# One copy of the last block's tail behind the join of the branches, and a new order in the one-lane block, in a fused WKV and two-layer mixture-of-experts kernel

## The chip, the cores and the metric

The kernel runs on one core of a Trainium2 chip. The metric is the device time of one execution in microseconds (us). The engines are called TensorE (PE in the profile, with its weight loads as PEld), VectorE (DVE), ScalarE (ACT), GpSimd (POOL) and SyncE (SP); the last two issue the transfers here, GpSimd those with indices (gathers and scatters) and SyncE the plain ones.

## What is computed

A recurrent attention gives one row per token; two mixture-of-experts (MoE) layers follow, each token going to the expert with the largest logit. The second layer has a capacity of 384 tokens per expert.

```python
# attention: B=2, H=8, S=768, D=48
for t in range(S):
    y[:, :, t] = einsum('bhd,bhde->bhe', rt, state + einsum('bhd,bhe->bhde', u * kt, vt))
    state = wt[..., None] * state + einsum('bhd,bhe->bhde', kt, vt)
x = y.transpose(0, 2, 1, 3).reshape(1536, 384)
# layer 0 (N=1536, D=384, E=8, F=1024)
logits = x @ w_gate + modality_bias[modality_id]
e = argmax(logits); gate = softmax(logits)[e]
x = gate * (relu(x @ w1[e]) @ w2[e])
# layer 1, without the bias, and with 384 places per expert
logits = x @ w_gate
e = argmax(logits); gate = softmax(logits)[e]
out = gate * (relu(x @ w1[e]) @ w2[e])   # 0 where the expert is full
```

## The kernel before

**Blocks.** In each layer a routing step sorts the tokens by expert into at most 13 blocks (NU) of two lanes of 128 rows. A block gathers its rows (`xg`), transposes them (`xp`, then the parts `xh` and `xl`), multiplies them with one expert's w1, takes the relu, multiplies with w2 into `y` (one PSUM tile per lane, `ykeep`), scales by the gate into a buffer `yo`, and scatters the rows to DRAM with an indirect DMA. Weights and activations are each split in two parts (h and l, `hi` at L960 and `lo` at L963) and three products are summed. The weights of block j+1 (`w1r`, `w2r` raw; `w1h`, `w1l`, `w2h`, `w2l` split) are split during block j: the high parts on ScalarE, the low parts on VectorE.

**Two forms.** A block whose two lanes share an expert has the form `two`; a block in which only its second lane has work has the form `one`. Here layer 0 has eight blocks: 0 to 5 are of form `two`, 6 and 7 of form `one`. Layer 1 has ten. The order of the work is written out by hand and is the same on each engine's queue; for `one` the table ONE lists by letters what stands behind which step: a to j are the pieces of the next block's weights (ScalarE and VectorE), `0` and `1` the relus of the two halves of F, `x` and `X` the transposes and casts of the next block's rows, `P` and `Q` the gate's softmax, and for the previous block's second lane `y` the transposes of its scaled row, `z` the two splits on VectorE, `l` its logits for layer 1 and then its store. The table RELU says on which engine the relu of each half runs.

**The outputs of layer 0.** A stored row of layer 0 holds the 384 values and 8 logits for layer 1's gate, which `yturn3`, `ysplit3` and `ylog3` work out from the scaled row. The second lane of block j is scaled, turned and stored only in block j+1 (from j = 5 on the scaling is the first ScalarE work of block j+1, L1127). The two buffers `yo` alternate with j.

**The end of layer 0.** How many blocks there are is known only at run time. `rest(j)` is a chain of tests: if there are more than j blocks, `body(j)` and `rest(j+1)`, else `last(j-1)`. Each of the possible ends has its own copy of `last`: a load of all rows' logits (`lgd`, L1337) on SyncE behind the stores, the load of layer 1's w2 of one expert (`w2r`, L913), the scaling of the last lane (L1343), its transposes (L1347), the copies (L1348), the logits (L696), a one-hot product that places them among the others (L1350, L1351), the store, and the add that gives layer 1's logits (L1354):

```python
nc.vector.tensor_add(lgs[1], lgs[0], pl)
```

Layer 1's routing starts from that sum, and its first gather needs the routing's result.

Of the kernel before, what the change touches and what calls it, by code (L numbers as in the profile page):

```python
# [27 lines left out]
E, F = 8, 1024  # L28
# [899 lines left out]
class MoePools:  # L928
    def __init__(self, tc, ctx, raw, run):
# [21 lines left out]
        self.gm = cp.tile([P, 2, 2], F32, name="gm")  # L951


def moe(tc, c, m, route, run, layer, src, w1d, w2d, dst, wg2, wp2, zb, following, lgs=None, psum=None, bad=None, general=None, ykeep=None):
# [21 lines left out]
    with ctx:  # L976
# [46 lines left out]
        def gates(j, part):  # L1023

            gd = m.gd[j % 2]
            if part == 0:
                lx = m.xg[j % 2][:, :, DM:XW]
                nc.vector.tensor_reduce(m.gm[:, 0], lx, AX.X, ALU.max)
                nc.vector.tensor_tensor(gd[:, :, 0:E], lx, m.gm[:, 0].unsqueeze(2).to_broadcast((P, 2, E)), ALU.subtract)  # L1029
            elif part == 1:  # L1030
                nc.scalar.activation(gd[:, :, 0:E], gd[:, :, 0:E], AF.Exp)
            else:

                nc.vector.tensor_reduce(m.gm[:, 1], gd, AX.X, ALU.add)
                nc.vector.reciprocal(R.gate[:, 2 * j : 2 * j + 2], m.gm[:, 1])
# [21 lines left out]
        def relu(j, half):  # L1057
# [3 lines left out]
            for a in range(0, 512, wd):  # L1061
                if RELU[half] == "s" or wd == 512:
# [61 lines left out]
        def scale(j, t, eng):  # L1124
            py = ykeep[t]
            if eng == "s":
                nc.scalar.activation(m.yo[j % 2][:, t, 0:DM], py, AF.Identity, scale=R.gate[:, 2 * j + t : 2 * j + t + 1])  # L1127
                return
            nc.vector.tensor_scalar(m.yo[j % 2][:, t, 0:DM], py, R.gate[:, 2 * j + t : 2 * j + t + 1], None, ALU.mult)

        def store(j, t):
            nc.gpsimd.indirect_dma_start(  # L1132
                out=dst, out_offset=bass.IndirectOffsetOnAxis(ap=R.ids[:, 2 * j + t : 2 * j + t + 1], axis=0),
                in_=m.yo[j % 2][:, t, 0:SO], in_offset=None, bounds_check=N - 1, oob_is_err=False,
            )

        def yturn3(j, t):
            pt = psum.tile([P, KD, P], F32, tag="tp", name=f"yt{j}{t}" + n, bufs=TP[layer])
            for kc in range(KD):
                nc.tensor.transpose(pt[:, kc], m.yo[j % 2][:, t, kc * P : (kc + 1) * P], c.ident)  # L1140
# [8 lines left out]
        def ylog3(j, t):  # L1149
            logits3(tc, psum, [m.yp], wp2, m.yo[j % 2][:, t : t + 1, DM:XW], f"_y{j}{t}" + n, "lg", 1)  # L1150
# [14 lines left out]
        def one(j, pc):  # L1165
# [3 lines left out]
            def work():  # L1169
                for p in next(plan):  # L1170
# [3 lines left out]
                    elif p == "y":  # L1174
                        if before:
                            if j < NU_MIN:
# [10 lines left out]
                    elif p == "s":  # L1187
                        if layer == 0 and j < NU_MIN - 1:
# [32 lines left out]
        def two(j, pc):  # L1221
            before = layer == 0 and j > 0
            first2(j, 0)
            if before:
                if j < NU_MIN:
# [44 lines left out]
            end = layer == 0 and j >= NU_MIN - 1  # L1270
# [3 lines left out]
            if layer == 0 and not end:  # L1274
# [48 lines left out]

        def last(j):
            if layer:
                finish(j)
            else:

                sp = ap.tile([P, 512], F32, tag="h0", name=f"sp{j}" + n, bufs=1)
                ohp, ohc = sp[:, 0:P], sp[:, P : P + NC]  # L1330
                put = sp[:, P + NC : P + NC * (E + 1)].rearrange("p (c e) -> p c e", e=E)
                col = slice(2 * j + 1, 2 * j + 2)
                nc.vector.tensor_scalar(ohp, c.i1[:, :, 0], R.tp[:, col], None, ALU.is_equal)
                nc.vector.tensor_scalar(ohc, c.jx[:, 0:NC], R.tc[:, col], None, ALU.is_equal)

                pl = psum.tile([P, NC, E], F32, tag="tp", name=f"lq{j}" + n, bufs=TP[0])
                nc.sync.dma_start(lgs[0], dst.rearrange("(p j) e -> p j e", j=NC)[:, :, DM:XW])  # L1337
                er = EXPERT0[j % 2]
                m.raw.load(j % 2, *following, slice(er, er + 1), parts=(1,))

                for kc in range(KD):
                    ks = slice(kc * P, kc * P + P)
                    nc.scalar.activation(m.yo[j % 2][:, 1, ks], ykeep[1][:, ks], AF.Identity, scale=R.gate[:, col])  # L1343
                xT = ap.tile([P, KD, P], F32, tag="lxT", name=f"lx{j}" + n, bufs=1)
                for kc in range(KD):
                    pt = psum.tile([P, P], F32, tag="h" if kc == 1 else "tp", name=f"yt{j}{kc}" + n, bufs=2 if kc == 1 else TP[0])
                    nc.tensor.transpose(pt, m.yo[j % 2][:, 1, kc * P : (kc + 1) * P], c.ident)  # L1347
                    nc.scalar.copy(xT[:, kc], pt)  # L1348
                py = logits(tc, psum, [xT[:, kc] for kc in range(KD)], wg2, None, None, f"_y{j}1" + n, "lg", 1)
                nc.vector.tensor_tensor(put, py.unsqueeze(1).to_broadcast((P, NC, E)), ohc.unsqueeze(2).to_broadcast((P, NC, E)), ALU.mult)  # L1350
                nc.tensor.matmul(pl, lhsT=ohp, rhs=put, start=True, stop=True)  # L1351
                nc.vector.tensor_copy(m.yo[j % 2][:, 1, DM:XW], py)
                store(j, 1)
                nc.vector.tensor_add(lgs[1], lgs[0], pl)  # L1354

                if j % 2 == 0:
                    for p in p0:
                        hi(p, nc.scalar)
                        lo(p, nc.vector)

        def rest(j):
# [140 lines left out]
```

## Time and profile before

| | |
|---|---|
| median of 3 runs | 452.43 us (452.07 to 452.55) |
| the profiled execution's own time | 451.07 us |
| its span, first to last instruction | 449.3 us |
| TensorE busy | 417.9 us, 93% |
| VectorE busy | 329.5 us, 73% |
| ScalarE busy | 249.3 us, 55% |
| layer 0's last block: first scaling, add behind it | 252.49 us, 273.28 us |

The times of single instructions come from the profiled execution, whose own time stands beside its span; the runs were timed without a profile. Blocks 6 and 7 of layer 0 lie between about 241 and 266 us.

### The profile page before, as it was taken

What the parts mean: (1) busy time and instruction counts of PE and PEld (TensorE: products, weight loads), DVE (VectorE), ACT (ScalarE), POOL (GpSimd) and SP (SyncE); (2) the same over time, 40 slices, a digit from 0 to 9 for tenths busy, and PEclk for the clock granted to TensorE, in tenths of its full rate; (3) what the DMA queues carried; (4) which work ended last, traced back from release to release, by engine and by line L of the source; (5) the groups of instructions that cost most, each with busy time, mean ns of one, the idle gap of its engine ahead of it and who ended that gap; (6) DMA issues with size and microseconds to landing.
All of it is one profiled execution on the core that took longest, in us unless ns stands there. A gap on an engine that the chain in (4) does not pass through costs nothing. (4 is left out here: it accounts for less than half of the span.)

```text
span 449.3 us, 9663 instructions
## 1 busy us (share of the span) xinstructions
PE 417.9 (93%) x3270; PEld 380.1 (85%) x3275; DVE 329.5 (73%) x677; ACT 249.3 (55%) x508; POOL 143.3 (32%) x160
## 2 busy tenths in 40 slices
PE   8999999999899999999999956999999999999990
PEld 4789988987389999999997854899899999998990
DVE  7798867984879859677597975386974945859760
ACT  3256545543537647557475840277864755777650
POOL 5637963141230422213223300503343132124420
PEclk9999999999899999999999996999999999999996
DMA  6987237348630121366744945314887657761100
GB/s 113 200 148 152 48 56 194 74 169 324 197 91 2 56 79 54 109 205 222 256 147 134 292 129 154 91 20 131 319 281 258 228 187 232 237 230 52 50 22 20
DMA packets 85590, 66.98 MB, mean 149 GB/s; under 512 B 60586, under 2 KB 77655, under 8 KB 85504
## 3 DMA queue, kind: packets, MB, share of 16 engines
q1 hardware_dynamic: 80512, 52.30, 39.8%
q0 software_dynamic: 4992, 13.61, 9.9%
q8 instruction: 44, 0.72, 0.7%
q14 instruction: 42, 0.34, 0.2%
HBM read 95.63 MB, written 11.56 MB: 239 GB/s over the span
## 5 line engine op out<-in xcount | busy, mean ns | idle before, releaser
L963 DVE TENSOR_TENSOR w1l<-w1r,w1h 128x512 fp32r<-128x512 f32 x114 | 71.7, 686 | 9.6 <-ACT w1h L960 9.4
L963 DVE TENSOR_TENSOR w2l<-w2r,w2h 128x768 fp32r<-128x768 f32 x76 | 69.2, 951 | 0.3 <-ACT w2h L960 0.3
L960 ACT CAST w1h<-w1r 128x512 fp32r<-128x512 f32 x114 | 62.7, 617 | 0.3 <-DMA xs<-zv 0.3
L1107 DVE SCALAR_TENSOR_TENSOR qhl_m<-qh_m,qhh_m 128x512 fp32r<-128x512 f32 x48 | 33.0, 686 | 36.0 <-ACT qhh_m L1106 36.0
L960 ACT CAST w2h<-w2r 128x768 fp32r<-128x768 f32 x76 | 59.4, 835 | 0.0
L1106 ACT ACTIVATE qhh_m<-qh_m 128x512 fp32r<-128x512 f32 x48 | 28.8, 599 | 41.7 <-PE qh_m L1101 41.7
L1101 PE MATMUL qh_m<-xh,w1h 128*128 128x256 f32 x288 | 51.0, 286 | 0.3 <-ACT xh L1318 0.2
L1101 PE MATMUL qh_m<-xl,w1h 128*128 128x256 f32 x288 | 50.2, 283 | 0.6 <-DVE w2l L963 0.6
L1119 PE MATMUL y_m<-w2h,qhh_m 128*128 128x384 f32 x192 | 50.0, 341 | 0.0
L1101 PE MATMUL qh_m<-xh,w1l 128*128 128x256 f32 x288 | 49.8, 282 | 0.0
L1119 PE MATMUL y_m<-w2l,qhh_m 128*128 128x384 f32 x192 | 49.6, 339 | 0.0
L1119 PE MATMUL y_m<-w2h,qhl_m 128*128 128x384 f32 x192 | 49.3, 338 | 0.0
L1004 POOL DMA_INDIRECT xg<-x,idg_l x24 | 26.0, 1083 | 69.2 <-DVE gd L1029 43.3
L1004 POOL DMA_INDIRECT xg<-xs,idg_l x20 | 22.2, 1111 | 67.2 <-issue 54.7
L1101 PEld LDWEIGHTS qh_m<-xh,w1h 128*128 128x128 f32 x288 | 42.6, 188 | 0.8 <-ACT xh L1318 0.8
L1101 PEld LDWEIGHTS qh_m<-xl,w1h 128*128 128x128 f32 x288 | 40.9, 188 | 1.2 <-DVE w2l L963 1.0
L1101 PEld LDWEIGHTS qh_m<-xh,w1l 128*128 128x128 f32 x288 | 40.9, 188 | 0.0
L1132 POOL DMA_INDIRECT out_dram<-yo,ids_l x20 | 22.1, 1103 | 49.3 <-ACT w2h L960 11.5
L1127 ACT ACTIVATE yo<-y_m,gate_l 128x384 f32<-128x384 f32 x29 | 16.9, 582 | 36.6 <-PE y_m L1119 28.9
L1020 ACT CAST xh<-xp_m 128x384 fp32r<-128x384 f32 x38 | 16.7, 485 | 35.8 <-PE xp_m L1019 35.8
L397 ACT ACTIVATE X<-endt,Sb 112x112 f32<-112x112 f32 x40 | 14.2, 354 | 38.5 <-PE endt L387 27.2
L1132 POOL DMA_INDIRECT x<-yo,ids_l x14 | 17.5, 1251 | 54.4 <-DVE qhl_m L1107 23.9
(252 smaller groups left out, 892.9 us busy)
## 6 DMA issues: line engine op xcount, KB each, us to landing
w2r<-in_moe_w_dram SPq DMA_DIRECT2D x50, 768.0 KB
w1r<-in_moe_w_dram SPq DMA_DIRECT2D x72, 512.0 KB
xs<-zv SPq DMA_DIRECT2D x12, 192.0 KB
out_dram<-zt SPq DMA_DIRECT2D x4, 576.0 KB
raw_w<-in_w_dram SPq DMA_DIRECT2D x14, 144.0 KB
raw_r<-in_r_dram SPq DMA_DIRECT2D x14, 144.0 KB
raw_k<-in_k_dram SPq DMA_DIRECT2D x14, 144.0 KB
raw_v<-in_v_dram SPq DMA_DIRECT2D x14, 144.0 KB
```

The source lines that it names most:

```text
L397: nc.scalar.activation(Xn, z, AF.Identity, scale=Tn)
L960: (eng.copy if eng is nc.scalar else eng.tensor_copy)(p[1], p[0])
L963: eng.tensor_sub(p[2], p[0], p[1].bitcast(F32))
L1004: nc.gpsimd.indirect_dma_start(out=m.xg[j % 2][:, t], out_offset=None, in_=src, in_offset=bass.IndirectOffsetOnAxis(ap=R.idg[:, 2 * j + t ...
L1020: nc.scalar.copy(m.xh[j % 2][:, :, ts], pt)
L1101: nc.tensor.matmul(ph[:, f], lhsT=w[s][:, kc, fs], rhs=a[s][:, kc], start=(i == 0), stop=(i == 3 * KD - 1))
L1106: nc.scalar.activation(hh, ph, AF.Relu)
L1107: nc.vector.scalar_tensor_tensor(hl, ph, 0.0, hh.bitcast(F32), ALU.max, ALU.subtract)
L1119: nc.tensor.matmul(st["y", j, t], lhsT=a[:, f, ts], rhs=w[s][:, 2 * q + f], start=(q == 0 and i == 0), stop=(q == 3 and i == 5))
L1127: nc.scalar.activation(m.yo[j % 2][:, t, 0:DM], py, AF.Identity, scale=R.gate[:, 2 * j + t : 2 * j + t + 1])
L1132: nc.gpsimd.indirect_dma_start(out=dst, out_offset=bass.IndirectOffsetOnAxis(ap=R.ids[:, 2 * j + t : 2 * j + t + 1], axis=0), in_=m.yo[j % ...
```

## The change

- The scaling, the transposes, the logits, the placing, the store and the add of the last block leave `last(j)` and stand once, in `ending()`, behind the join of all branches. What differs by the last block's number stays in the branch: the two one-hot rows, a copy of the row numbers (`idl`), the read-back `lgd` and the load of layer 1's w2.
- So that one piece of code can serve every last block, the second lane of all blocks from 5 on (TAIL) uses one buffer, yo[1][:, 1], and one pair of gates, `gl`. The one-hot tile takes the place of yo[0][:, 1].
- Each test now has the end on its first side and the next block on its second.
- In layer 0 the relu of the second half moves from VectorE to ScalarE (RELU). In the `one` form `x` and `X` come ahead of the second half's transposes, `z` behind them, and `l` and `Q` behind the first half of the second product.
- Block 5's first-lane logits and store move from its own end into block 6.

```diff
-RELU = "sv"
+
+TAIL = NU_MIN - 1
+RELU = ("ss", "sv")
-ONE = (('ecadfPyz', '01bQ', 'X', 'l', 'hgix', 'js'), ('badec0P', 'f1hQ', 'xX', 'i', 'j', 'g'))
+ONE = (('ecadfPy', '01b', 'xX', 'z', 'lQhgi', 'js'), ('badec0P', 'f1hQ', 'xX', 'i', 'j', 'g'))
...
+        def YO(j, t):
+            return m.yo[1][:, 1] if t and layer == 0 and j >= TAIL else m.yo[j % 2][:, t]
+
+        def GATE(j):
+            return m.gl if layer == 0 and j >= TAIL else R.gate[:, 2 * j : 2 * j + 2]
...
-            py = ykeep[t]
+            py, to, by = ykeep[t], YO(j, t)[:, 0:DM], GATE(j)[:, t : t + 1]
             if eng == "s":
-                nc.scalar.activation(m.yo[j % 2][:, t, 0:DM], py, AF.Identity, scale=R.gate[:, 2 * j + t : 2 * j + t + 1])
+                nc.scalar.activation(to, py, AF.Identity, scale=by)
...
-                            if j < NU_MIN:
+                            if j <= NU_MIN:
                                 ylog3(j - 1, 0)
...
-            end = layer == 0 and j >= NU_MIN - 1
+            end = layer == 0 and j >= NU_MIN
...
         def last(j):
+
             if layer:
                 finish(j)
-            else:
...
+                return
+            col = slice(2 * j + 1, 2 * j + 2)
+            nc.vector.tensor_scalar(ohp, c.i1[:, :, 0], R.tp[:, col], None, ALU.is_equal)
+            nc.vector.tensor_scalar(ohc, c.jx[:, 0:NC], R.tc[:, col], None, ALU.is_equal)
+            nc.vector.tensor_copy(m.idl, R.ids[:, col])
+            if j < NU_MIN:
+                ylog3(j, 0)
+            nc.sync.dma_start(lgs[0], dst.rearrange("(p j) e -> p j e", j=NC)[:, :, DM:XW])
+            er = EXPERT0[j % 2]
+            m.raw.load(j % 2, *following, slice(er, er + 1), parts=(1,))
...
+        def ending():
+
+
+            yl = YO(NU, 1)
+            for kc in range(KD):
+                ks = slice(kc * P, kc * P + P)
+                nc.scalar.activation(yl[:, ks], ykeep[1][:, ks], AF.Identity, scale=m.gl[:, 1:2])
...
+            nc.vector.tensor_add(lgs[1], lgs[0], pl)
...
-            with tc.If(nblk > j) as cmp:
+
+            with tc.If(nblk < j + 1) as cmp:
+                last(j - 1)
+            with cmp.Else():
                 body(j)
                 rest(j + 1)
-            with cmp.Else():
-                last(j - 1)
 
         rest(NU_MIN)
+        if layer == 0 and run == "":
+            ending()
```

ScalarE at the start of block 7, before: `yo0` is the output buffer, `y1` the PSUM tile of the second lane, and a name in `waits` is a counter of an engine or of a DMA queue (DMASW of GpSimd's transfers, DMAHW of SyncE's).

```order
L1000 TENSOR_LOAD kind_l0_1742
L1127 ACTIVATE yo0_1636<-y1_m0_1762,gate_l0_1747 128x384 [waits DMASW1_49,DVE_49,PE_49]
L1295 COMPARE_AND_BRANCH
L960 CAST w1h0_1622<-w1r0_87 128x512 [waits DMAHW3_49]
L960 CAST w1h0_1622<-w1r0_87 128x512 [waits DMAHW4_49]
L960 CAST w1h0_1622<-w1r0_87 128x512 [waits DMAHW2_49]
L960 CAST w1h0_1622<-w1r0_87 128x512 x2
L1031 ACTIVATE gd1_1643<-gd1_1643 128x2x8 [waits DVE_49]
```

The same place after the change.

```order
L1004 TENSOR_LOAD kind_l0_1744
L1137 ACTIVATE yo1_1637<-y1_m0_1764,gl_1645 128x384 [waits DVE_49,DMASW5_49,PE_49,Activation_49]
L1305 COMPARE_AND_BRANCH
L964 CAST w1h0_1622<-w1r0_87 128x512 [waits DMAHW3_49]
L964 CAST w1h0_1622<-w1r0_87 128x512 [waits DMAHW4_49]
L964 CAST w1h0_1622<-w1r0_87 128x512 [waits DMAHW2_49]
L964 CAST w1h0_1622<-w1r0_87 128x512 x2
L1035 ACTIVATE gd1_1643<-gd1_1643 128x2x8 [waits DVE_49]
```

The opening scaling now writes `yo1` and waits for another store's counter (DMASW5 for DMASW1).

ScalarE in the middle of block 7, before: `hp` are the transposed relus, `xp80` and `xp81` the next block's rows.

```order
L1063 ACTIVATE h70_m0_4972<-ph70_m0_4923 128x512
L960 CAST w1h0_1622<-w1r0_87 128x512
L1075 CAST hh70_m0_4986<-hp70_m0_4981 128x512 [waits PE_49]
L1020 CAST xh0_1632<-xp81_m0_4990 128x3x128 [waits PE_49]
L1075 CAST hh71_m0_5001<-hp71_m0_4996 128x512 [waits PE_49]
L960 CAST w2h0_1626<-w2r0_89 128x768 [waits DMAHW5_49]
L960 CAST w2h0_1626<-w2r0_89 128x768
L960 CAST w2h0_1626<-w2r0_89 128x768 [waits DMAHW6_49]
L1020 CAST xh0_1632<-xp80_m0_5037 128x3x128 [waits PE_49]
L960 CAST w2h0_1626<-w2r0_89 128x768
```

After, from the first relu on.

```order
L1073 ACTIVATE h70_m0_5032<-ph70_m0_4985 128x512
L1073 ACTIVATE h71_m0_5034<-ph71_m0_5013 128x256 [waits PE_49]
L1073 ACTIVATE h71_m0_5034<-ph71_m0_5013 128x256
L964 CAST w1h0_1622<-w1r0_87 128x512
L1085 CAST hh70_m0_5044<-hp70_m0_5039 128x512 [waits PE_49]
L1024 CAST xh0_1632<-xp80_m0_5048 128x3x128 [waits PE_49]
L1024 CAST xh0_1632<-xp81_m0_5054 128x3x128 [waits PE_49]
L1085 CAST hh71_m0_5065<-hp71_m0_5060 128x512 [waits PE_49]
L964 CAST w2h0_1626<-w2r0_89 128x768 [waits DMAHW5_49]
L964 CAST w2h0_1626<-w2r0_89 128x768
```

Both x casts now stand between the two hh casts, where one stood, and the second half's relu, in two pieces, stands ahead of the weight piece that follows the first relu.

VectorE at the end of layer 0, before, in the branch that runs here (`lgd` is the read-back, `lq7` the placed logits).

```order
L1333 TENSOR_SCALAR sp7_m0_14545<-i1_756,tp_l0_1755 128x128
L1334 TENSOR_SCALAR sp7_m0_14545<-jx_758,tc_l0_1756 128x12
L1350 TENSOR_TENSOR sp7_m0_14545<-lpl_y71_m0_14565,sp7_m0_14545 128x96 [waits DVE_49,PE_49]
L1352 COPY yo1_1637<-lpl_y71_m0_14565 128x8 [waits DMASW5_49]
L1354 TENSOR_TENSOR lg2_1612<-lgd_81,lq7_m0_14548 128x96 [waits DMAHW1_49,PE_49]
L1372 UNCONDITIONAL_BRANCH [waits DVE_sequencer_49]
```

After, behind the join (the first row is the end of the last branch's weights).

```order
L967 TENSOR_TENSOR w2l0_1628<-w2r0_89,w2h0_1626 128x768 [waits Activation_49]
L1387 UNCONDITIONAL_BRANCH [waits DVE_sequencer_49]
L1372 TENSOR_TENSOR yo0_1636<-lpl_y_m0_14330,yo0_1636 128x96 [waits DMASW4_49,DVE_49,PE_49]
L1374 COPY yo1_1637<-lpl_y_m0_14330 128x8 [waits DMASW4_49,DMASW5_49,DMASW2_49,DMASW7_49,DMASW1_49,DMASW0_49]
L1379 TENSOR_TENSOR lg2_1612<-lgd_81,lq_m0_14319 128x96 [waits DMAHW5_49,DMAHW4_49,DMAHW6_49,DMAHW3_49,DMAHW7_49,DMAHW1_49,PE_49]
L747 TENSOR_REDUCE mx_l1_14345<-lg2_1612 128x12 [waits DVE_49]
```

The add, L1354 before and L1379 after, waited for TensorE and one counter of SyncE and now waits for TensorE and six.

## Rows read from the trace of the kernel before

**Rows 1.** The page: its head, and TensorE's row (busy us, share, instructions).

```profile
span 449.3 us, 9663 instructions
...
PE 417.9 (93%) x3270; PEld 380.1 (85%) x3275; DVE 329.5 (73%) x677; ACT 249.3 (55%) x508; POOL 143.3 (32%) x160
```

**Rows 2.** Timeline of ScalarE: start us, us, line, operation, count, idle before.

```profile
244.48 0.60 ACT L1063 ACTIVATE h_m<-ph_m 128x512 f32<-128x512 f32 x1
...
246.63 0.59 ACT L1075 CAST hh_m<-hp_m 128x512 fp32r<-128x512 f32 x1 [1.03 <-PE hp_m L1072]
247.11 0.49 ACT L1020 CAST xh<-xp_m 128x384 fp32r<-128x384 f32 x1
...
252.49 0.58 ACT L1127 ACTIVATE yo<-y_m,gate_l 128x384 f32<-128x384 f32 x1 [0.90 <-PE y_m L1088]
252.97 2.69 ACT L960 CAST w1h<-w1r 128x512 fp32r<-128x512 f32 x5
...
255.68 0.46 ACT L1142 CAST yp<-yt_m 128x384 bf16<-128x384 f32 x1
...
267.15 0.88 ACT L1343 ACTIVATE yo<-y_m,gate_l 128x128 f32<-128x128 f32 x3 [3.09 <-DVE w2l L963]
```

**Rows 3.** Timeline of VectorE.

```profile
245.47 0.36 DVE L1146 CAST yp<-yr_m 128x384 bf16<-128x384 f32 x1
245.86 0.56 DVE L1147 TENSOR_TENSOR yp<-yr_m,yp 128x384 bf16<-128x384 f32 x1
246.33 0.75 DVE L1065 TENSOR_SCALAR h_m<-ph_m 128x256 f32<-128x256 f32 x2
...
248.93 0.68 DVE L1076 TENSOR_TENSOR hl_m<-hp_m,hh_m 128x512 fp32r<-128x512 f32 x1
249.53 0.17 DVE L723 TENSOR_REDUCE yo<-l_y_m 128x8 f32<-128x24 f32 x1
...
273.28 0.26 DVE L1354 TENSOR_TENSOR lg<-lgd,lq_m 128x96 f32<-128x96 f32 x1 [0.76 <-PE lq_m L1351]
```

**Rows 4.** Timeline of GpSimd: the stores of blocks 5 and 6, layer 1's first gather.

```profile
250.48 1.02 POOL L1132 DMA_INDIRECT x<-yo,ids_l  x1 [5.24 <-ACT w2h L960]
...
263.00 1.02 POOL L1132 DMA_INDIRECT x<-yo,ids_l  x1 [5.24 <-ACT w2h L960]
...
281.32 1.05 POOL L1004 DMA_INDIRECT xg<-x,idg_l  x1 [7.01 <-DVE fu_l L858]
```

**Rows 5.** Timeline of TensorE.

```profile
245.87 0.28 PE L1053 MATMUL ph_m<-w1l,xh 128*128 128x256 f32 x1
...
247.41 0.38 PE L722 MATMUL l_y_m<-wp,yp 128*128 128x24 bf16 x9
...
259.32 0.77 PE L1072 MATMUL hp_m<-ident,h_m 128*128 128x128 f32 x4 [1.56 <-DVE h_m L1065]
...
270.92 1.24 PE L696 MATMUL lpl_y_m<-wg,lx_m 128*128 128x8 f32 x6 [2.49 <-issue]
```

**Rows 6.** Landing of stores issued in 250-251, 262.5-264 and 230-246 us (two).

```profile
DMA to landing us min/median/max: 5.7/5.7/5.7
...
DMA to landing us min/median/max: 4.7/4.7/4.7
...
DMA to landing us min/median/max: 3.2/4.7/6.2
```

**Rows 7.** Timeline of SyncE's queue, and the transfers' size.

```profile
267.69 0.60 SPq L1337 DMA_DIRECT2D lgd<-x  x1
268.43 2.37 SPq L913 DMA_DIRECT2D w2r<-in_moe_w_dram  x2
...
w2r<-in_moe_w_dram SPq DMA_DIRECT2D x2, 768.0 KB
```

**Rows 8.** Windows: length, busy us (instructions) by engine, clock, DMA share, GB/s.

```profile
272.00:276.00 4.00, 2.97 (x11) 1.52 (x13) 2.36 (x10) 0.00 (x0) 1.00 (x1) 0.50 1.04 388
276.00:277.00 1.00, 1.00 (x5) 0.33 (x4) 0.93 (x6) 0.00 (x0) 0.00 (x0) 0.65 0.17 58
```

More of the change, by code (lines that the diff above doesn't have):

```diff
@@ L951, in __init__ @@
         self.gm = cp.tile([P, 2, 2], F32, name="gm")
+        self.gl = cp.tile([P, 2], F32, name="gl")
+        self.idl = cp.tile([P, 1], I32, name="idl")
 def moe(tc, c, m, route, run, layer, src, w1d, w2d, dst, wg2, wp2, zb, following, lgs=None, psum=None, bad=None, general=None, ykeep=None):
@@ L1061, in relu @@
             for a in range(0, 512, wd):
-                if RELU[half] == "s" or wd == 512:
+                if RELU[layer][half] == "s" or wd == 512:
                     nc.scalar.activation(h[:, a : a + wd], ph[:, a : a + wd], AF.Relu)
@@ L1149, in ylog3 @@
         def ylog3(j, t):
-            logits3(tc, psum, [m.yp], wp2, m.yo[j % 2][:, t : t + 1, DM:XW], f"_y{j}{t}" + n, "lg", 1)
+            logits3(tc, psum, [m.yp], wp2, YO(j, t)[:, DM:XW].unsqueeze(1), f"_y{j}{t}" + n, "lg", 1)
             store(j, t)
@@ L1187, in work @@
                     elif p == "s":
-                        if layer == 0 and j < NU_MIN - 1:
+                        if layer == 0 and j < TAIL:
                             scale(j, 1, "s")
@@ L1224, in two @@
             if before:
-                if j < NU_MIN:
+                if j <= NU_MIN:
                     ylog3(j - 1, 0)
@@ L1273, in two @@
             second2(j, 3, 1, (lambda: ylog3(j, 0), 4) if end else None)
-            if layer == 0 and not end:
+            if layer == 0 and j < TAIL:
                 scale(j, 1, "s")
@@ L1322, in moe @@
         nblk = nc.values_load(R.ctl[0:1, 2 * NU : 2 * NU + 1], min_val=0, max_val=NU * P)
+        sp = m.yo[0][:, 1]
+        ohp, ohc = sp[:, 0:P], sp[:, P : P + NC]
+        put = sp[:, P + NC : P + NC * (E + 1)].rearrange("p (c e) -> p c e", e=E)
         def last(j):
@@ L1326, in last @@
                 finish(j)
-            else:
[L1329 to L1359, printed above, removed]
@@ new lines, in last @@
+            if j % 2 == 0:
+                for p in p0:
+                    hi(p, nc.scalar)
+                    lo(p, nc.vector)
+        def ending():
[3 more added lines that the diff above has]
+                nc.scalar.activation(yl[:, ks], ykeep[1][:, ks], AF.Identity, scale=m.gl[:, 1:2])
+            pl = psum.tile([P, NC, E], F32, tag="tp", name="lq" + n, bufs=TP[0])
+            xT = ap.tile([P, KD, P], F32, tag="lxT", name="lx" + n, bufs=1)
+            for kc in range(KD):
+                pt = psum.tile([P, P], F32, tag="h" if kc == 1 else "tp", name=f"yt{kc}" + n, bufs=2 if kc == 1 else TP[0])
+                nc.tensor.transpose(pt, yl[:, kc * P : (kc + 1) * P], c.ident)
+                nc.scalar.copy(xT[:, kc], pt)
+            py = logits(tc, psum, [xT[:, kc] for kc in range(KD)], wg2, None, None, "_y" + n, "lg", 1)
+            nc.vector.tensor_tensor(put, py.unsqueeze(1).to_broadcast((P, NC, E)), ohc.unsqueeze(2).to_broadcast((P, NC, E)), ALU.mult)
+            nc.tensor.matmul(pl, lhsT=ohp, rhs=put, start=True, stop=True)
+            nc.vector.tensor_copy(yl[:, DM:XW], py)
+            nc.gpsimd.indirect_dma_start(
+                out=dst, out_offset=bass.IndirectOffsetOnAxis(ap=m.idl, axis=0),
+                in_=yl, in_offset=None, bounds_check=N - 1, oob_is_err=False,
+            )
+            nc.vector.tensor_add(lgs[1], lgs[0], pl)
```

8 lines of the change are left out of this document (4 added, 4 removed).

## The prediction, made before the changed kernel was run

> **What bounds the kernel now.** I read the page first: a span of 449.3 us with TensorE busy for 93% of it [rows 1]. Over most of the program a change off TensorE is therefore hidden. The change, however, touches the end of layer 0, and there I read the timelines engine by engine from 240 us on. In that place TensorE is not the bound: the last block's tail is a chain through ScalarE (three scalings from 267.15 us [rows 2]), TensorE, VectorE and the queues of SyncE and GpSimd, and layer 1's routing cannot begin before the chain's last step, the add at L1354 (273.28 us [rows 3]). Behind the add come only the routing and the gathers that need its result, the first of them at 281.32 us [rows 4], and then ten blocks of layer 1, whose order the change leaves as it is. So a microsecond at the add is a microsecond at the end of the kernel, and the question is when the add can run.
>
> Two waits that the changed program has and the old one has not decide it. Their places are the two order listings under the change: the scaling that opens block 7 on ScalarE, and the add behind the join on VectorE.
>
> **First wait: the scaling of block 6's second lane.** Before, block 7's first ScalarE instruction (L1127) writes buffer yo0 and waits for a store of two blocks back. It ran at 252.49 us [rows 2]. After, it writes yo1, as all second lanes from block 5 on do, and so waits until the store of block 5's second lane has read that buffer (DMASW5). When is that store done?
>
> *Its issue.* Before, GpSimd issued it at 250.48 us [rows 4], 0.78 us behind the end of the reduction at 249.53 + 0.17 = 249.70 us [rows 3]. After, the pieces ahead of it are in another order, and ScalarE carries both relus. TensorE's last matmuls of the second half stand at 245.87 us [rows 5], so the second 256-wide relu ends near 246.6 us (I give a 256-wide one 0.4 us, between the 512-wide one's 0.60 us [rows 2] and nothing). Behind it on ScalarE, with the durations of [rows 2]: a weight cast (2.69 / 5 = 0.54), hh of the first half (0.59), two x casts (0.49 each, both now ahead of the second hh), hh of the second half (0.59): 249.3 us. Then VectorE [rows 3]: hl 0.68, the two splits 0.36 and 0.56, which now stand behind hl, so 250.9 us. Then the logits matmuls 0.38 [rows 5], the reduction 0.17, and 0.78 to the issue: 252.2 us, 1.7 us later than before.
>
> *Its landing.* The trace has four stores of this kind in this part, with 3.2, 4.7, 5.7 and 6.2 us to landing [rows 6]. I take their mean, 4.95 us: 257.2 us. So the scaling starts 4.7 us later than at 252.49. Bounds: 255.4 us (+2.9) and 258.4 us (+5.9).
>
> *What is queued behind it.* On ScalarE: five weight casts (2.69 us [rows 2]), the exponential, the yp cast, all three relus, hh and x. On TensorE: the transposes of the scaled lane. From this scaling to the issue of block 6's second store it took 263.00 - 252.49 = 10.5 us [rows 2, 4]. Adding up the new ScalarE order (0.58 + 2.69 + 0.46 + 0.60 + 0.8 + 0.54 + 0.59 + 0.98 + 0.59 = 7.8; steps overlap by some 0.1 us, as the casts starting at 252.97 do with the scaling that ends at 253.07, and the short exponential is left out, so I take 7.2) and the same VectorE tail (0.68 + 0.36 + 0.56 + 0.38 + 0.17 + 0.78 = 2.9) gives 10.1 us. The 1.56 us that TensorE waited for VectorE's relu in block 7 [rows 5] is the slack that makes it shorter. So this store is issued at 267.3 us, +4.3. Before, SyncE could read the logits back (lgd, L1337) when this store had landed: 263.00 + 4.7 = 267.7, and it did so at 267.69 us [rows 4, 6, 7]. After: 272.0 us, again +4.3.
>
> **Second wait: the add behind the join.** Before, in its own branch, the add waited for TensorE and for one of SyncE's counters, the read-back. After, it stands where the branches have joined, and the listing shows six of SyncE's counters. One of them belongs to the last load that SyncE issues in the branch: layer 1's w2 weights, two pieces of 768 KB [rows 7], issued right behind the read-back. Before, nothing needed them here. From the windows they move at 388 GB/s until 276 us and still 58 GB/s in the next microsecond [rows 8], so I let them end at 277.0 us: 9.3 us behind the read-back's issue. The add came 5.6 us behind it. After, it cannot come before 272.0 + 9.3 + 0.1 = 281.4 us, which is 8.1 us later than 273.28. The tail itself does not decide: the first scaling behind the join waits for the landing too (near 272.6 us), and from there to the add it took 6.1 us before, of which 2.49 us was an idle TensorE [rows 5]; that ends near 276.5 us, well ahead of the weights. Bounds of this term: if the load ended at 276.2 us, 0.8 us less.
>
> **What it removes, and why that gives nothing.** VectorE loses two relus of 0.75 us in all per block (blocks 6 and 7, [rows 3]); ScalarE gets them. Block 5 loses nine logits matmuls (0.38 us [rows 5]), which block 6 now does. TensorE's 2.49 us "issue" ahead of L696 [rows 5] goes, since the tail is no longer in a far branch. All of these lie ahead of the two waits, which end 4 to 8 us later than what the removed pieces held up, so they are worth nothing here. Without the waits the 2.49 us would be gain.
>
> On that idle time the Trainium skill (Runtime: NRT & Kernel Launch, section Instruction fetch mechanics) has a rule that speaks against the gain: a taken branch whose target lies outside the pages already fetched has to fetch its page before execution goes on. The 2.49 us ahead of L696 agree in size with such a fetch, and by the rule it is moved and not removed, since block 7's short branch now jumps over five unused blocks to the join. If the engines met it there in the open, the sum would be 2.5 us more; the trace's own reading is that it falls into their 5 us and more of waiting.
>
> Layer 1's code is the same but for which side of each test its blocks stand on; its blocks keep TensorE busy, and I take 0, with 0.5 us either way.
>
> **Sum.** +4.3 (read-back later) + 3.8 (the add for the weights) = +8.1 us. The profiled execution took 451.07 us by its own time (span 449.3), so it would be 459.2. The median of the runs, 452.43, is 0.3% above it; on that scale the forecast is 460.5 us.
>
> **The rivals.**
> - *Both waits bite* (the forecast): chance 0.72. With its own bounds (landings from 3.2 to 6.2 us, the load's end) it lies between +5.7 and +10.2: 458.1 to 462.6.
> - *Only the weights' wait*: the first store lands before block 7 wants its buffer, or the old pace survives because ScalarE catches up. The read-back stays at 267.69, the add runs at 277.1: +3.8, 456.2. For it: one of the four stores landed in 3.2 us. Against: even that gives 255.4, and 252.49 is wanted. Chance 0.10.
> - *Only the buffer's wait*: the add's list is long, but the weights are in time, as they would be if they did not share the engines with the read-back. The tail ends at 276.5: +3.2, 455.6. Against: 1.57 MB at 388 GB/s alone is 4 us, and before it took 9.3. Chance 0.08.
> - *Faster*: neither wait bites, and TensorE's idle 2.49 us is gone: -2.5, 449.9; with VectorE's relus off the path (1.56) as much as -4.1, 448.3. It decides if block 5's store lands within about half a microsecond of its issue, or the counters stand for earlier transfers than I read, and the weights land 4 us sooner. No row shows a landing under 3.2 us. Chance 0.05.
> - *Slower still*: in the idle stretches of block 7 and of the join TensorE's granted clock falls further than before. It is 0.50 (the lower of its two levels, 1.2 GHz) in 272 to 276 us already [rows 8]. Block 7's work behind the first wait is some 9 us; a third of it at half clock is +3: 463.5. Chance 0.05.
>
> **How the numbers follow.** A measurement of this kernel tells about 0.2% (0.9 us) from no change. All cases but "faster" lie over that; between them a mixture (a hidden wait set off by the removed idle time) could land within it, for which I leave 0.03, out of the second and third. Faster 0.05, same 0.03, slower 0.92. The range runs from the second case (456.0) to the upper bound of the first (462.6); it leaves out the third, the fourth and the last, 0.18 together.
>
> **What would show it.** Right: in block 7 ScalarE's first scaling is idle for some 4 us with the store as its releaser; GpSimd's second store in block 7 lies near 267 us; the add follows a wait of about 4 us for SyncE's w2r load, with TensorE's matmul in front of it long done; the routing behind it has the same length as before. Wrong: the scaling starts right behind block 6's last matmul (first wait), or the add right behind TensorE's one-hot matmul (second wait). I would be off in size if the store of block 5 is issued earlier than 252.2 us because ScalarE's new order runs more tightly than I add it up, or if landings come nearer to 3 than to 5 us when less else is moved.

## The result and the profile after

The changed kernel took 459.9 us in the median (457.57 to 460.48, six runs), the kernel before 452.91 us (452.07 to 454.48) beside it: a ratio of 1.0141, interval 1.0111 to 1.0171 (ratios go by the mean times, here 459.55 and 453.17). The forecast was 460.5 us, slower by 8.1. The profiled execution took 459.61 us by its own time.

```profile
span 457.8 us, 9662 instructions
```

ScalarE's timeline around block 7 of layer 0 (block 6 opens at 239.13, block 7 at 255.76, the tail behind the join at 271.97).

```profile
239.13 0.58 ACT L1137 ACTIVATE yo<-y_m,gl 128x384 f32<-128x384 f32 x1 [1.22 <-PE y_m L1129]
...
255.76 0.58 ACT L1137 ACTIVATE yo<-y_m,gl 128x384 f32<-128x384 f32 x1 [5.04 <-DMA x<-yo,ids_l]
...
271.97 0.88 ACT L1364 ACTIVATE yo<-y_m,gl 128x128 f32<-128x128 f32 x3 [5.03 <-DMA xg<-xs,idg_l]
```

The first wait is in the middle row: ScalarE stands idle for 5.04 us, and what releases it is a store, where in [rows 2] it was TensorE after 0.90 us. Next GpSimd's timeline: the stores of block 5 (both lanes), of block 6, of block 7, and layer 1's first gather.

```profile
244.56 1.02 POOL L1142 DMA_INDIRECT x<-yo,ids_l  x1 [0.59 <-ACT h_m L1073]
252.06 1.59 POOL L1142 DMA_INDIRECT x<-yo,ids_l  x1 [6.48 <-DVE w2l L967]
...
267.91 1.27 POOL L1142 DMA_INDIRECT x<-yo,ids_l  x1 [10.81 <-ACTq L1393]
281.55 1.05 POOL L1375 DMA_INDIRECT x<-yo,idl  x1 [12.38 <-DVE eq_l L748]
288.50 1.05 POOL L1008 DMA_INDIRECT xg<-x,idg_l  x1 [5.89 <-DVE fu_l L860]
```

SyncE's queue and VectorE's timeline show the second wait.

```profile
270.82 0.60 SPq L1349 DMA_DIRECT2D lgd<-x  x1
271.54 1.59 SPq L915 DMA_DIRECT2D w2r<-in_moe_w_dram  x2
```

```profile
249.71 0.18 DVE L725 TENSOR_REDUCE yo<-l_y_m 128x8 f32<-128x24 f32 x1 [0.33 <-PE l_y_m L724]
...
266.95 0.18 DVE L725 TENSOR_REDUCE yo<-l_y_m 128x8 f32<-128x24 f32 x1 [1.36 <-PE l_y_m L724]
...
276.06 0.26 DVE L1372 TENSOR_TENSOR yo<-lpl_y_m,yo 128x96 f32<-128x96 f32 x1 [4.73 <-PE lpl_y_m L698]
276.33 0.17 DVE L1374 COPY yo<-lpl_y_m 128x8 f32<-128x8 f32 x1
280.56 0.25 DVE L1379 TENSOR_TENSOR lg<-lgd,lq_m 128x96 f32<-128x96 f32 x1 [4.07 <-DMA w2r<-in_moe_w_dram]
```

The add had waited 0.76 us for TensorE [rows 3]; it now waits 4.07 us, and its releaser is the load of weights (`w2r`), which it does not read. It lies 9.74 us behind the read-back, 5.59 us before.

TensorE has two rows that the forecast did not have: in block 7 four like matmuls of w2 take 1.63 us, and at the start of layer 1 its row of 60 warming matmuls (work that only keeps TensorE busy) is broken by gaps. First the block, then layer 1.

```profile
263.03 1.63 PE L1098 MATMUL y_m<-w2h,hh_m 128*128 128x384 f32 x4
...
288.52 3.06 PE L757 MATMUL warm_m<-i,ones 128*128 128x128 bf16 x51
292.02 0.33 PE L757 MATMUL warm_m<-i,ones 128*128 128x128 bf16 x3 [0.44 <-issue]
292.75 0.27 PE L757 MATMUL warm_m<-i,ones 128*128 128x128 bf16 x2 [0.40 <-issue]
293.46 0.22 PE L757 MATMUL warm_m<-i,ones 128*128 128x128 bf16 x1 [0.44 <-issue]
294.18 0.34 PE L757 MATMUL warm_m<-i,ones 128*128 128x128 bf16 x3 [0.50 <-issue]
294.55 0.52 PE L1023 MATMUL xp_m<-ident,xg 128*128 128x128 f32 x3
...
296.43 0.72 PE L1111 MATMUL qh_m<-xh,w1h 128*128 128x256 f32 x3
```

The last row is layer 1's first product with w1, which before stood here:

```profile
287.53 0.66 PE L1101 MATMUL qh_m<-xh,w1h 128*128 128x256 f32 x3 [0.20 <-ACT xh L1318]
```

The windows give the clock that goes with block 7's four matmuls (the last three columns are the granted clock, the DMA share and GB/s; 1.00 is the higher of the two levels, 2.4 GHz).

```profile
260.00:264.00 4.00, 2.93 (x17) 2.69 (x18) 2.73 (x6) 2.80 (x8) 0.00 (x0) 0.81 0.51 188
264.00:268.00 4.00, 4.00 (x27) 3.84 (x26) 2.53 (x7) 2.93 (x5) 0.09 (x1) 0.76 0.02 4
```

Put together, from one profiled execution each: block 7's opening scaling +3.27 us (255.76 against 252.49); from there to block 6's second store 12.15 us, 10.51 before (+1.64); from that store to the read-back 2.91 us, 4.69 before (-1.78); from the read-back to the add +4.15. Sum: the add comes 7.28 us later. Then from the add to the gather 7.94 us, 8.04 before (-0.10), and from the gather to layer 1's first transposes 6.05 us, where the kernel before needed 3.4 us (+2.7). Of these 2.7 us, 1.0 is given back before the first product with w1: it comes 8.90 us later (296.43 against 287.53). The span grew by 8.5 us.

### The profile page after: what moved, and what is told of

The parts are those of the page before. It is cut to its first block, busy times and chain, and to the rows that moved or that the text cites. A ratio compares the mean times of both kernels' runs of the same rounds, so it can differ in the third digit from the quotient of the medians.

```text
span 457.8 us, 9662 instructions
## 1 busy us (share of the span) xinstructions
PE 421.7 (92%) x3275; PEld 381.8 (83%) x3275; DVE 328.5 (72%) x674; ACT 249.3 (54%) x512; POOL 144.6 (32%) x160
## 5 line engine op out<-in xcount | busy, mean ns | idle before, releaser
L1142 POOL DMA_INDIRECT out_dram<-yo,ids_l x20 | 23.5, 1176 | 49.9 <-ACT w1h L964 14.0
L1129 PEld LDWEIGHTS y_m<-w2h,qhl_m 128*128 128x128 f32 x192 | 34.8, 188 | 0.0
L1129 PEld LDWEIGHTS y_m<-w2l,qhh_m 128*128 128x128 f32 x192 | 34.4, 188 | 0.1
```

What stands on the lines that cost most here:

```text
L1129: nc.tensor.matmul(st["y", j, t], lhsT=a[:, f, ts], rhs=w[s][:, 2 * q + f], start=(q == 0 and i == 0), stop=(q == 3 and i == 5))
L1142: nc.gpsimd.indirect_dma_start(out=dst, out_offset=bass.IndirectOffsetOnAxis(ap=R.ids[:, 2 * j + t : 2 * j + t + 1], axis=0), in_=YO(j, t) ...
```

## The experiments

Chips differ by a few microseconds, so every kernel is compared by its ratio to the kernel before on its own chip; the changed kernel has 1.0141.

**The first wait undone.** The second lanes alternate between the buffers again, and the tail has buffers of its own.

```diff
-            return m.yo[1][:, 1] if t and layer == 0 and j >= TAIL else m.yo[j % 2][:, t]
+            return m.ye if j == NU else m.yo[j % 2][:, t]
-        sp = m.yo[0][:, 1]
+        sp = m.sp
```

> The changed kernel with the second lanes of blocks 5 and on in alternating buffers again; the tail behind the join has a buffer of its own, and the one-hot rows too. The theory (two waits): ScalarE's opening scaling of block 7 starts right behind TensorE's product of block 6, near 252 us and not at 255.8, the read-back goes out some 4 us earlier than at 270.8, the add still waits for the weights about 9.7 us behind the read-back: near 276.5; the kernel takes 455 to 456.5 us (changed kernel 459.9, before 452.9). Rival (the buffer's wait is hidden, only the weights matter): the read-back stays within 1 us of 270.8 and the time within 1 us of 459.9.

Measured 1.0039 (1.002 to 1.0059), 455.23 us. The scaling starts at 250.81 us with TensorE as its releaser, the read-back goes out at 265.97, and the add comes 9.39 us behind it (9.74 in the changed kernel).

```profile
250.81 0.58 ACT L1139 ACTIVATE yo<-y_m,gl 128x384 f32<-128x384 f32 x1 [1.16 <-PE y_m L1100]
```

```profile
275.36 0.25 DVE L1381 TENSOR_TENSOR lg<-lgd,lq_m 128x96 f32<-128x96 f32 x1 [5.04 <-issue]
...
L1381 DVEq EVENT_SEMAPHORE  x3: 50/50/5111, 270.0 to 275.3; - x3
```

The timeline names no releaser ("issue"). The second row is another view, of line L1381 in VectorE's sequencer (DVEq), the part of the engine that checks counters and takes branches: number of instructions, shortest/median/longest in ns, first and last start. One of the add's three checks of counters took 5.11 us, as one of them took 3.95 us in the changed kernel, so the add still stands at SyncE's counters.

The first wait is worth 1.0% (1.0141 less 1.0039, some 4.6 us); the rival, that it is hidden, falls.

**The second wait undone, in two ways.** One copies the read-back in the branch, so that the add needs no load:

```diff
             nc.sync.dma_start(lgs[0], dst.rearrange("(p j) e -> p j e", j=NC)[:, :, DM:XW])
+            nc.vector.tensor_copy(lgs[1], lgs[0])
...
-            nc.vector.tensor_add(lgs[1], lgs[0], pl)
+            nc.vector.tensor_add(lgs[1], lgs[1], pl)
```

> The changed kernel with one VectorE copy of the read-back in the branch, so that the add behind the join needs TensorE alone; the weights are still loaded behind the read-back, and GpSimd's last store still waits for all of SyncE's loads. The theory: the add runs near 276.6 us and not at 280.6, but the store still goes out near 281.5 us and layer 1's first gather, which reads what it stores, waits for its landing (3 to 5 us): the gather moves from 288.5 to 285 or 286, and the kernel takes 457 to 458 us. Rival (the add alone holds layer 1): the gather moves by 4 us, 456 us. Second rival (the wait for the weights was not what held the add): 459.9.

Measured 1.0153 (1.0116 to 1.0191): nothing gained. The time is the second rival's, but not for its reason. VectorE's timeline and two rows of its sequencer show why.

```profile
273.67 0.21 DVE L1350 COPY lg<-lgd 128x96 f32<-128x96 f32 x1 [2.83 <-DMA lgd<-x]
280.02 0.26 DVE L1373 TENSOR_TENSOR yo<-lpl_y_m,yo 128x96 f32<-128x96 f32 x1 [6.14 <-issue]
...
L1394 DVEq COMPARE_BRANCH  x2: 47/48/50, 267.7 to 273.8; - x2
L1373 DVEq EVENT_SEMAPHORE  x1: 50/50/50, 279.9 to 279.9; - x1
```

The copy made VectorE leave its branch at 273.8 us, with the weights in flight. The next thing that VectorE does at all is a check of counters at 279.9 us, and that check takes only 0.05 us. So the 6.1 us between are no wait for a counter; they lie between the branch instruction and what stands behind it. The other way takes the read-back out of the branch, so that the weights go out ahead of it:

```diff
-            nc.sync.dma_start(lgs[0], dst.rearrange("(p j) e -> p j e", j=NC)[:, :, DM:XW])
...
         def ending():
+            nc.sync.dma_start(lgs[0], dst.rearrange("(p j) e -> p j e", j=NC)[:, :, DM:XW])
```

> The changed kernel with the read-back issued once behind the join, and layer 1's weights alone in the branch, so ahead of it. The theory: the weights go out near 258 us, while block 7 runs, and are there long before the add; the read-back goes out when block 6's store has landed (near 271 us), the add and the last store come behind the one-hot product, near 276.6 us, and the kernel takes 455.5 to 456.5 us. Rival (the read-back itself, many small pieces, is what takes the time): the add stays near 280 us, and the kernel within 1 us of 459.9.

Measured 1.0038 (1.002 to 1.0056), 456.04 us. The weights leave at 256.74 us, the add comes right behind TensorE:

```profile
256.74 2.43 SPq L915 DMA_DIRECT2D w2r<-in_moe_w_dram  x4
272.09 0.61 SPq L1360 DMA_DIRECT2D lgd<-x  x1
```

```profile
275.74 0.25 DVE L1379 TENSOR_TENSOR lg<-lgd,lq_m 128x96 f32<-128x96 f32 x1 [0.65 <-PE lq_m L1373]
```

So the second wait, too, is worth 1.0%, and it is the weights, not the small pieces of the read-back, that it stood for.

**Both undone.** Both edits in one kernel.

> Both edits, alternating buffers with a buffer of its own for the tail, and the weights ahead of the read-back behind the join. The theory: the two waits add up, so the add comes near 271 to 272 us, ahead of the 273.3 us of the kernel before, and the kernel takes 450 to 452.5 us: the rest of the change (relu, order, no far branch) then shows as a gain of 0.5 to 3 us over before. Rival (the rest of the change is itself worth nothing or costs): 453 us or more.

Measured 0.9979 (0.9956 to 1.0003): the two waits are all of the loss, and the rest of the change is within what can be told from nothing. The add is at 274.30 us and not at 271 to 272. TensorE, done with block 7 at 264.34, does its next instruction 6.55 us later:

```profile
270.89 0.90 PE L1371 MATMUL yt_m<-ident,ye 128*128 128x128 f32 x3 [6.55 <-issue]
```

```profile
264.00:266.00 2.00, 0.34 (x2) 0.02 (x1) 2.00 (x3) 0.00 (x0) 0.41 (x1) 1.00 1.06 398
```

In that time it leaves the branch for the join, while the early weights move at 398 GB/s. The row of TensorE's sequencer (PEldq) shows that one branch instruction took 6.15 us of it:

```profile
L1395 PEldq COMPARE_BRANCH  x2: 65/3108/6152, 263.8 to 264.7; - x2
```

To tell the jump from the weights, the same kernel without that load (so that one expert of layer 1 is computed with old weights):

```diff
-            er = EXPERT0[j % 2]
-            m.raw.load(j % 2, *following, slice(er, er + 1), parts=(1,))
```

> Both waits undone, and the load of layer 1's w2 weights in the branch left out, so that one expert of layer 1 is computed with old weights. Both waits undone, TensorE needed 6.2 us for the jump to the join while those weights moved at 398 GB/s, and ScalarE 5.0 us. Theory (the jump has to fetch code, and the fetch stands behind the weights): TensorE's first transposes behind the join come 2 to 3 us earlier against the end of block 7's product, and the ratio is 0.991 to 0.995. Rival (the jump takes that long anyway): 0.997 to 0.999.

Measured 0.9932 (0.9911 to 0.9954), 450.46 us. From the end of block 7's product (264.83) to TensorE's first transposes it is 4.33 us now, and the branch instruction takes 3.93 us of it. The timeline names ScalarE as the releaser, whose first scaling had ended at 268.47 us; the branch, from 265.2 us on, ended last:

```profile
269.16 0.55 PE L1369 MATMUL yt_m<-ident,ye 128*128 128x128 f32 x3 [4.33 <-ACT ye L1364]
...
L1393 PEldq COMPARE_BRANCH  x2: 65/1998/3930, 264.2 to 265.2; - x2
```

ScalarE itself stood for 4.40 us "issue" (5.00 with the weights). So TensorE's jump to the join takes some 4 us here without the weights, and 2 us more in the execution in which they move. That is one execution of each: with everything undone (below) the same branch took 4.69 us, begun in the middle of the weights as well (365 and 328 GB/s in 262 to 266 us).

A jump to the tail is nothing new, however. In the kernel before, TensorE's branch to its own copy of the tail took 4.70 us:

```profile
L1372 PEldq COMPARE_BRANCH  x2: 291/2496/4701, 262.9 to 272.7; - x2
```

It began at 262.9 us, 2.0 us before block 7's last product ended (264.05 + 0.86 = 264.91), so only 2.85 us of it showed as idle time. Behind the join the long branch begins at 265.2 us, when the last product (264.83) has ended, and lies in the open.

**The order alone, and the old order.** The tables RELU and ONE of the kernel before in the changed kernel:

> The changed kernel with the tables RELU and ONE of the kernel before; all else as changed, the two new waits too. Theory: the order makes the stores of blocks 5 and 6 later than they need be (their splits and logits stand behind more work), so block 5's store goes out near 250.5 us and not at 252.1, the scaling that waits for it starts some 1.5 us earlier, and the kernel takes 1 to 2.5 us less than the changed kernel: ratio to before 1.009 to 1.012 (changed kernel 1.014). Rival (the new order is a gain that the waits hide): ratio 1.014 or more.

Measured 1.0067 (1.0041 to 1.0093), but not for the reason given: the scaling of block 7 stays at 255.63 us. GpSimd's and VectorE's timelines and the first store's landing:

```profile
244.26 1.02 POOL L1142 DMA_INDIRECT x<-yo,ids_l  x1 [0.59 <-issue]
251.94 1.08 POOL L1142 DMA_INDIRECT x<-yo,ids_l  x1 [6.66 <-DVE xl L1025]
```

```profile
248.04 0.17 DVE L725 TENSOR_REDUCE yo<-l_y_m 128x8 f32<-128x24 f32 x1
```

```profile
DMA to landing us min/median/max: 6.9/6.9/6.9
```

The second store's logits are there at 248.21 us, and it goes out at 251.94: 0.78 us behind the landing of the first one (244.26 + 6.9 = 251.16). It waits for that store. What the old order gives comes later, in block 7: 9.79 us from the scaling to the second store, 12.15 in the changed kernel (how much of that is the order, the part on the prediction says); the row of warming matmuls has no gaps here either. The tables of the change alone in the kernel before:

> The kernel before with the new tables RELU and ONE alone: tail in the branches, alternating buffers, no new wait. Theory: the later store of block 6 makes the read-back later by 0.5 to 2 us: ratio 1.001 to 1.004. Rival (VectorE rid of two relus per block and TensorE of its 1.6 us wait): ratio 0.996 to 0.999.

Measured 1.0013 (0.9994 to 1.0032): not to be told from nothing. The trace has block 6 longer by 1.8 us (240.66 to 254.25, 252.49 before) and the step from block 7's scaling to its store 0.9 us longer (11.39, 10.51 before), of which the tail gives back a part. No gain from the relus shows.

**Block 5's logits.** Their move alone, in the kernel before:

```diff
-            end = layer == 0 and j >= NU_MIN - 1
+            end = layer == 0 and j >= NU_MIN
...
-                if j < NU_MIN:
+                if j <= NU_MIN:
                     ylog3(j - 1, 0)
```

> The kernel before with block 5's first-lane logits and store moved to block 6 alone. In the changed kernel block 6's opening scaling ran at 239.1 us and not at 240.7, 1.5 us earlier. Theory (this move is what gave it): it runs near 239.1 us here too, and the lead is kept to the end of layer 0, since nothing there waits for more: ratio 0.995 to 0.998. Rival (the lead comes from before block 5 and is not of the move, or block 6 gives it back): ratio 0.999 to 1.001.

Measured 0.9907 (0.9875 to 0.9939), 446.19 against 450.33 us: faster than both kernels, and by more than expected. Block 6's opening scaling ran at 239.94 us and not near 239.1: the step from block 5's opening scaling to it is 3.43 us, 4.11 before, which is 0.7 us. More came from a place that the edit does not name: TensorE's tail.

```profile
267.63 0.80 PE L1349 MATMUL yt_m<-ident,yo 128*128 128x128 f32 x3 [3.20 <-ACT yo L1345]
268.29 0.89 PE L696 MATMUL lpl_y_m<-wg,lx_m 128*128 128x8 f32 x6
```

```profile
270.70 0.26 DVE L1356 TENSOR_TENSOR lg<-lgd,lq_m 128x96 f32<-128x96 f32 x1 [1.16 <-DMA lgd<-x]
```

The 2.49 us of idle TensorE at L696 [rows 5] are gone, and the add comes at 270.70 us, 2.6 us earlier than before. The same work stands there, so I took it for the place of the instructions, and tried that in the kernel before with eight idle matmuls:

```diff
+                if j == 7:
+                    shift = psum.tile([P, 512], F32, tag="h", name="shift" + n, bufs=2)
+                    for _ in range(8):
+                        nc.tensor.matmul(shift[:, 0:128], lhsT=c.ones, rhs=c.i1.rearrange("p a b -> p (a b)")[:, 0:128].bitcast(BF16), start=True, stop=True)
```

> The kernel before with eight small matmuls more on TensorE ahead of the last block's transposes, where TensorE waits for ScalarE; they compute nothing and only shift the logits matmuls (L696) in TensorE's program. Theory: the 2.49 us of idle TensorE between the first and the second of six like weight loads at L696 is the program's place in memory, as the gaps of layer 1 were; it goes, the add comes near 270.8 us and not at 273.3, as with block 5's logits moved (270.7), and the ratio is 0.993 to 0.996. Rival (the idle time belongs to the work there): the ratio is 0.998 to 1.002.

Measured 0.9963 (0.994 to 0.9986), between the two ranges. L696 has no idle time ahead of it, but the add comes 5.68 us behind the first scaling (6.13 before): at 272.29 us and not near 270.8.

```profile
268.63 0.61 PE L1344 MATMUL shift_m<-i,ones 128*128 128x128 bf16 x8 [3.45 <-issue]
269.07 0.60 PE L1351 MATMUL yt_m<-ident,yo 128*128 128x128 f32 x3
269.71 1.45 PE L696 MATMUL lpl_y_m<-wg,lx_m 128*128 128x8 f32 x6
```

The stall is gone when the instructions are shifted, as the theory has it; part of it came back ahead of the eight matmuls (3.45 us idle, 2.85 there before), so the gain at the add is less than the 2.5 us. That the place makes the stall is likely and not shown: of the fourteen traces only that of the kernel before has it, and that kernel was profiled once. The opposite edit, block 5's logits back in the changed kernel:

> The changed kernel with block 5's first-lane logits and store back at the end of block 5; both new waits stay. In the changed kernel GpSimd issued block 5's second store only when the first, moved into block 6, had landed (244.6 + 6.9 us). Theory: that store comes earlier again by about 1.5 us although block 6 starts 1.5 us later, so the scaling that waits for it comes near 255 us; block 6's later start and the earlier store nearly cancel: ratio 1.009 to 1.014 (some of it for the gaps of layer 1, which go when the program is shifted). Rival (the second store waits for its own logits): it comes later by 1.5 us, scaling near 257, ratio 1.016 or more.

Measured 1.0185 (1.0137 to 1.0233), not clear of the changed kernel's 1.0141. The second store now goes out 0.79 us behind its own logits (250.43, 251.22), no longer behind the first store; counted from block 6's opening (238.74 us here) that is 12.48 us against 12.93. The logits come later and the first store earlier, so the move made that store only 0.45 us later. Block 7's scaling runs at 255.02 us, near 255 as the theory had it. The ratio does not fall as expected, although the add comes at 278.38 us, 2.2 us earlier than in the changed kernel; the gaps of layer 1 are in this kernel too.

**The gaps at layer 1's start.** Ten idle matmuls on TensorE behind the join in the changed kernel:

> The changed kernel with ten small matmuls more on TensorE behind the join, while it waits there; they shift what follows in TensorE's program by 20 instructions and compute nothing. In all kernels with the tail behind the join TensorE's row of warming matmuls at the start of layer 1 is broken by three or four gaps of 0.4 to 1.2 us from its 51st to 53rd matmul on, and the first transposes of layer 1 come 5.9 to 6.2 us behind the first gather, 3.4 us in the kernel before. Theory (the gaps go with the place in the program's memory): they start about 10 matmuls earlier in that row, or go. Rival (they go with what happens at that time, gathers or weights): they start at the 51st to 53rd again. Time: within 0.3% of the changed kernel's ratio of 1.014, or about 0.006 less if the gaps go.

Measured 1.0125 (1.0095 to 1.0155), not to be told from the changed kernel's 1.0141. The gaps were gone:

```profile
286.37 3.51 PE L757 MATMUL warm_m<-i,ones 128*128 128x128 bf16 x60
289.72 0.50 PE L1023 MATMUL xp_m<-ident,xg 128*128 128x128 f32 x3
```

But other kernels say that the place is not the cause: with block 5's logits back, with all undone (ten idle matmuls again), and in the kernel before with the eight matmuls, the code is shifted too, and the gaps stand at the 50th to 53rd matmul as ever. What the gaps go with is the chip. The experiments ran on three: the four kernels profiled on this run's chip (old order, tables alone, block 5's logits, this one) have none, and all eight profiled on the other two have them, the kernel before with eight matmuls among them. The kernel before, too, is faster on this run's chip: 450.33 us in the median against 453.4 and 454.23. So the gaps may well belong to the chip and not to the change, and then the ratios, taken on one chip each, hold little of them. In all nine kernels that have them SyncE's rows of the first w1 load of layer 1 take more than 2 us; in the five that have none (the kernel before among them) they take about 1.3 us. What stops both engines stays open.

**All undone.** Both waits undone, the old tables, and ten idle matmuls:

> The tail once behind the join, with alternating buffers and a buffer of its own, the weights ahead of the read-back, the tables RELU and ONE of the kernel before, and ten small matmuls that shift TensorE's program. Theory (both waits, the order and the gaps are what the change cost; the tail in one place is itself worth no loss): 2 to 4 us less than with both waits undone alone (ratio 0.998), so 0.989 to 0.994. Rival (TensorE's 6 us for the jump to the join, with the weights in flight, bounds it): 0.994 to 0.998.

Measured 0.9988 (0.9965 to 1.0011): not the theory, and a little over the rival's range. The gaps did not go in this kernel. The old order brings block 7 forward, but ScalarE and TensorE then stand at the jump for longer (TensorE 5.19 us):

```profile
268.35 0.88 ACT L1369 ACTIVATE ye<-y_m,gl 128x128 f32<-128x128 f32 x3 [6.12 <-issue]
```

## Why the prediction was right

*The forecast case held.* Both waits stand in the trace with the releasers that the prediction named, a store and the weights' load; each, undone alone, gives back 1.0%, and both together put the kernel at 0.998 of the one before.

*The sum, part by part.* The read-back came 3.13 us later for a forecast of 4.3, the add 7.28 us later for 8.1. The profiled execution, 459.61 us against a forecast of 459.2, is nearer than its parts by luck: behind the add it lost 1.3 us that the sum did not have. The outer bounds of the first case, +5.7 and +10.2, do not follow from the terms named there: landings of 3.2 and 6.2 us and 0.8 us of the load give +5.5 and +9.3.

*First wait, its issue: the right time by a wrong step.* Forecast 252.2 us, measured 252.06. The chain that I added up ended earlier than forecast, since block 6 opened 1.5 us sooner: the reduction ran at 249.71 where the sum had 251.3. The store then waited 2.17 us and not 0.78 for something that the sum lacked, the landing of block 5's first store, which the change had moved into block 6. I had counted that move as nine matmuls and not the store with it.

*Its landing: mis-sized.* The scaling followed the store's issue by 3.70 us, not by the mean of 4.95, so the wait was +3.3 us for a forecast of +4.7. The next store's landing was shorter too: the read-back came 2.91 us behind its issue, not 4.7.

*What is queued behind it: mis-sized the other way.* From the scaling to block 6's second store it was 12.15 us, not 10.1. Two kernels have the same order and the same first wait with the clock at 1.00 throughout: with the ten idle matmuls (255.21 to 265.95) and with block 5's logits back (255.02 to 265.76) the step is 10.74 us. The rows of the first of them:

```profile
262.21 0.95 PE L1098 MATMUL y_m<-w2h,hh_m 128*128 128x384 f32 x4
...
260.00:264.00 4.00, 2.93 (x21) 2.69 (x20) 3.11 (x6) 3.17 (x7) 0.00 (x0) 1.00 0.35 136
264.00:268.00 4.00, 3.15 (x25) 2.57 (x23) 3.60 (x9) 2.01 (x3) 1.27 (x1) 1.00 0.07 20
```

So 1.4 us of the step goes with the clock, which windows of 2 us show at 0.62 and 0.53, near the lower of its two levels (1.2 GHz), from 262 to 266 us in the changed kernel; that is the "slower still" rival in small. Just before, TensorE had waited 1.07 us for VectorE, and so it had in the two kernels whose clock stayed up; why it fell here is open. The order costs 0.95 us: with the old order, the same wait and full clock it is 9.79 us. The sum of durations had the order gain 0.4.

*Second wait: +4.15 for +3.8.* Its size and its releaser were right. That the copy in the branch did not help shows that there is more to it than the add's list of counters: VectorE, which left its branch while the weights moved, lost 6.1 us between its branch and the next instruction. That the weights made this long is argued, from TensorE's 6.15 us with them and 3.93 us without.

*What it removes: a wrong reading, hidden by the waits.* I had it at nothing, and in the changed kernel that held. But I read the 2.49 us at L696 as the price of the far branch. The trace of before has that branch elsewhere, ahead of the transposes, with 4.70 us; the 2.49 us come behind it, between the first and the second of six like weight loads. They go with the tail in one place, and also from the kernel before with eight idle matmuls, while the branch stays: 4.23 us in the changed kernel, 3.93 us and 6.15 us with both waits undone, and now in the open. That is what keeps the tail in one place from being a gain. The Trainium skill (Runtime: NRT & Kernel Launch, section Instruction fetch mechanics) says that a taken branch to a page not at hand has to fetch it first; branches of some 4 us in both kernels agree with that, but no run here shows which page was at hand, and the 2.49 us lie behind no branch.

*Layer 1: not 0.* In the profiled execution the gaps put the first transposes off by 2.7 us and the first product with w1 by 1.7 us. That the change made them is not shown, since they go with the chip. The premise that a microsecond at the add is one at the end holds only roughly: from the add to the last instruction the fourteen profiled executions took 173.9 to 179.8 us, and the kernel with block 5's logits back had its add 2.2 us earlier than the changed kernel and a span 0.4 us longer. The add explains 7.3 us of the span's 8.5; the medians differ by 7.0.

## What to carry to other kernels

Moving shared work behind the join of branches saves code, but everything that the branches have in flight becomes a condition of it: read, for each instruction behind a join, which transfers its list of waits takes in that it does not need, and issue those early or after. One buffer where there were two ties a writer to the last reader's transfer; when that reader is a scatter, count the landing, and the landing of the scatter ahead of it. A gain that an edit brings should be looked for in the trace where it was expected, since shifting code on TensorE alone moved this kernel by 0.4%. A stretch that differs between two traces should first be looked for on the same chip: here the gaps at the start of layer 1 went with the chip in all twelve experiments.

## What the runs showed that I had not expected

The branch instruction that jumps to the tail took TensorE 4.70 us in the kernel before, 3.93 us behind the join with little traffic and 6.15 us with weights at 398 GB/s; VectorE lost 6.1 us at its own in the middle of such a load. The timeline shows none of this as work: it is idle time put down to "issue" or to another engine, and only the rows of the sequencer name it. In the kernel before, 2.49 us of idle time lie between the first and the second of six like weight loads, and with eight matmuls ahead of them they are not there. Block 5's second store stood ready for 3.7 us (its logits done at 248.21, its issue at 251.94) behind the landing of a store to other rows of the same tensor.
